# An RWKV-6 attention and squared-ReLU MLP kernel whose engines' order is planned anew

## The chip, the cores and the metric

The kernel runs on one core of a Trainium2 chip. The metric is device time in microseconds, the median of several executions. The core's engines are TensorE (PE, matmuls), VectorE (DVE), ScalarE (ACT), GpSimd (POOL) and SyncE (SP, which here issues every DMA transfer). Each engine works through its own list of instructions strictly in the order written; an instruction that waits holds up everything behind it on that engine.

## What is computed

A recurrent attention (4 batches, 8 heads, 768 time steps, head size 48) and behind it a two-layer network on its 3072 rows of 384 numbers:

```python
for t in range(S):
    cur = np.einsum('bhd,bhe->bhde', u[None] * kt, vt)
    y[:, :, t] = np.einsum('bhd,bhde->bhe', rt, state + cur)
    state = wt[:, :, :, None] * state + np.einsum('bhd,bhe->bhde', kt, vt)
x = y.transpose(0, 2, 1, 3).reshape(B * S, H * D)
r = np.maximum(x @ w_in, 0.0)        # w_in 384 x 2048
out = (r * r) @ w_out                # w_out 2048 x 384
```

All inputs and the output are float32.

## The kernel before

**Tiling.** The 768 time steps of a batch are cut into 6 chunks of 128, so there are 24 steps, numbered 0 to 23. A step handles all 8 heads of one chunk. The recurrence within a chunk becomes matrix products, and between the chunks of one batch a state S is handed on. Every batch starts with an empty state, so steps 0, 6, 12 and 18 have none to wait for.

**What a step does.** Each word below is a function that issues one or a few instructions. `ld:s:w`, `:r`, `:k`, `:v` load the step's four inputs (lines 149 to 165, 192 KB each). `lw` takes the logarithm of w (ACT, line 248); `cum` sums it over time by a matmul into the PSUM tile cp (line 276); `ci` makes the negated inclusive sum from it (DVE, line 282; steps 0 to 2 have a second matmul instead); `exp` exponentiates both halves (ACT, line 289); `rd` multiplies r and k by them (DVE, line 299). `tr` transposes the result (8 matmuls, line 308), `rkt` copies it out of PSUM, `p` forms the products of r and k (line 327), `pm0` and `pm1` mask them (DVE, line 339). `su`, `ac`, `ts` and `sn` bring the state forward (PE lines 350 to 357, ACT line 295, DVE line 362, the last on DVE or POOL). `ku`, `qp`, `q` and `vq` form the term with u. `ys` and `ye` are the matmuls that make the output y (lines 376, 387), `ysb` adds the u term (DVE, line 392), `yt` transposes (line 400), and `xt` copies the step's 128 columns into the big bf16 tile xT.

**The network.** The weights come in 4 groups each: `ld:g:i` and `ld:g:o` load 768 KB of w_in or w_out in float32 into one of six staging tiles w_st (lines 174 to 184), and `cast:i:g:j`, `cast:o:g:j` convert a piece to bf16. The tokens are handled in 17 blocks: blocks 0 to 8 and 16 hold one step, blocks 9 to 15 hold two. `m1:i:g` is a group of 12 matmuls of 128 columns, or 6 of 256, that fills one PSUM bank (line 418); `rl` takes the scaled ReLU out of it (ACT line 427 or DVE line 429), and `gt` squares it: on ACT (line 439), on DVE (line 441), or, with the letter W, on DVE from the ReLU and the bank itself (line 436). `m2:i:mt:q` is a quarter of the second product for 128 rows (4 matmuls of 384 columns, line 462); `os` scales it into an output tile and `store` writes it out. `oh` and `sh` do this for the last rows, in two pieces, and the last `m2` is split in two column ranges (line 458). `warm:n` issues matmuls on zeros that nobody reads (line 481).

**What sets the order.** The whole program is one list of 1125 words, `ORDER`, lines 16 to 98. A word's last letter says on which engine a movable step runs (A for ACT, V and W for DVE, G for POOL). The words are called one after the other under a manual schedule, so each engine's own list is the list's words of that engine, in that order:

```python
    with tc.manual_schedule(engines={E.PE, E.DVE, E.Activation, E.Pool, E.SP}):
        for word in ORDER.split():
            name, *args = word.split(":")
            todo[name](*(int(a) if a.isdigit() else a for a in args))
```

**What an engine can wait for.** Besides data, it is a buffer whose last reader is not done. The ones that matter here are few:

```python
    a_in = ctx.enter_context(tc.tile_pool(name="a_in", bufs=A_IN))            # 7 steps of inputs
    ps_cp = ctx.enter_context(tc.tile_pool(name="ps_cp", bufs=1, space=PSUM)) # cum, p
    ps_tr_pool = ctx.enter_context(tc.tile_pool(name="ps_tr", bufs=1, space=PSUM)) # tr, su, yt
    ps_m1 = ctx.enter_context(tc.tile_pool(name="ps_m1", bufs=2, space=PSUM)) # m1, warm
    ps_m2 = ctx.enter_context(tc.tile_pool(name="ps_m2", bufs=2, space=PSUM)) # m2
```

An `m1` therefore starts when the `rl` (and, with W, the `gt`) of the `m1` before the last has read its bank; a `tr`, `su` or `yt` starts when the one before it in the list has been read out.

## Time and profile before

| | us |
|---|---|
| runs of the kernel before | 191.91, 192.04, 192.87 |
| their median | 192.04 |
| the profiled execution | 193.03 |
| its span, first to last instruction | 191.2 |
| PE, DVE, ACT, POOL busy in it | 183.3, 153.5, 143.1, 81.0 |

The span is that of one profiled execution; 1.83 us of its time lie outside the span. "Busy" is the time that an engine's instructions cover; instructions of one engine overlap a little, and the end of a matmul is modelled, so a busy PE may still be waiting inside a row. L427 and the like are lines of the kernel.

### The profile page before, as it was taken

To read this page: it belongs to the slowest core of one execution; us is meant where nothing else is said; L and a number is where in the kernel's file an instruction comes from. 1 tells how busy PE (TensorE), PEld (TensorE's weight loads), DVE (VectorE), ACT (ScalarE), POOL (GpSimd) and SP (SyncE) were. 2 spreads that over 40 slices of the span, in tenths; PEclk is the share of its full clock that TensorE was granted. 3 is DMA by queue.
4 is the path that set the end of the run, shared out by engine and by line. 5 is a ranking of instruction groups with operands and counts; after the bars stand their busy time and mean duration, and the time that the engine had idled before them with its cause. 6 is when DMAs were issued, how large, how long until landed. Compare 5 with 4: busy or idle time off the path is not lost.

```text
span 191.2 us, 5444 instructions
## 1 busy us (share of the span) xinstructions
PE 183.3 (96%) x2172; PEld 139.1 (73%) x2172; DVE 153.5 (80%) x283; ACT 143.1 (75%) x283; POOL 81.0 (42%) x110
## 2 busy tenths in 40 slices
PE   7898799999999999999999999999999999999993
PEld 2345598877789778778869768778778778778773
DVE  3599887867999989999899989986688957967360
ACT  3554399995869979798969779958969968666530
POOL 6268274524377897925471484850032120000000
PEclk9999999999999999999999999999999999999999
DMA  6999989999999998999999899402002011002012
GB/s 131 218 222 258 367 229 332 373 186 219 186 249 191 195 211 167 249 212 242 213 238 227 168 241 184 141 3 82 3 0 82 3 41 46 0 2 86 0 45 82
DMA packets 107179, 30.24 MB, mean 158 GB/s; under 512 B 100369, under 2 KB 105618, under 8 KB 107154
## 3 DMA queue, kind: packets, MB, share of 16 engines
q1 hardware_dynamic: 107154, 29.89, 66.5%
q8 instruction: 17, 0.28, 0.6%
q14 instruction: 8, 0.07, 0.1%
HBM read 25.17 MB, written 4.72 MB: 156 GB/s over the span
## 4 chain that ended last, share of the span: by engine, by line
PE 80%; SPq 7%; ACT 6%; DMA 4%; issue 1%; DVE 0%; ACTq 0%
PE m L462 31%; PE m L418 31%; SPq L150 6%; PE tr L308 5%; DMA w_st<-in_moe_w_in_dram 4%; PE cp L327 3%; ACT rl L427 3%; PE y L387 2%; PE tr L400 2%; PE cp L276 2%; PE y L376 1%; PE tr L353 1%; ACT gt L439 1%; PE m L458 1%; ACT wi_sb L187 1%
## 5 line engine op out<-in xcount | busy, mean ns | idle before, releaser
L418 PE MATMUL m<-xT,wi_sb 128*128 128x128 bf16 (+1 forms) x816 | 74.7, 241 | 1.3 <-ACT wi_sb L187 0.9
L462 PE MATMUL m<-wo_sb,gt 128*128 128x384 bf16 x368 | 70.8, 326 | 0.0
L418 PEld LDWEIGHTS <-wi_sb 128*128 128x128 bf16 x816 | 59.5, 98 | 8.9 <-ACT wi_sb L187 1.1
L427 ACT ACTIVATE rl<-m 128x512 f16<-128x512 f32 x76 | 44.2, 596 | 13.7 <-PE m L418 12.7
L462 PEld LDWEIGHTS <-gt 128*128 128x128 bf16 x368 | 33.1, 98 | 16.5
L439 ACT ACTIVATE gt<-rl 128x512 bf16<-128x512 f16 x56 | 34.4, 630 | 1.6 <-DVE rl L429 0.9
L339 DVE TENSOR_TENSOR pmT<-cp,tri_strict 128x512 bf16<-128x512 f32 x42 | 27.2, 683 | 1.4 <-PE cp L327 1.3
L299 DVE TENSOR_TENSOR rdec_buf<-rk_raw,cp 128x768 bf16<-128x768 f32 x24 | 22.7, 948 | 4.7 <-ACT cp L289 4.5
L289 ACT ACTIVATE cp<-cp 128x768 f32<-128x768 f32 x24 | 19.2, 801 | 7.6 <-DVE cp L282 4.5
L190 POOL TENSOR_TENSOR qprod<-rk_raw,ku 128x384 f32<-128x384 f32 x19 | 19.6, 1033 | 11.4 <-DVE ku L190 5.4
L190 POOL TENSOR_TENSOR vq<-v_raw,q 128x384 f32<-128x384 f32 x20 | 16.9, 842 | 14.9 <-DVE q L264 7.9
L190 POOL TENSOR_TENSOR ku<-rk_raw,u_bc 128x384 f32<-128x384 f32 x19 | 20.2, 1064 | 0.3 <-issue 0.3
L190 POOL TENSOR_TENSOR S<-t_state,ac_buf 128x384 bf16<-128x384 f32 x11 | 9.4, 853 | 23.3 <-DVE t_state L362 23.3
L441 DVE TENSOR_TENSOR gt<-rl 128x512 bf16<-128x512 f16 x31 | 13.8, 447 | 6.4 <-ACT rl L427 6.3
L392 DVE TENSOR_TENSOR y_sb<-vq,y 128x384 bf16<-128x384 f32 x24 | 13.1, 548 | 4.0 <-PE y L387 4.0
L187 ACT COPY rkT<-tr 128x1024 bf16<-128x1024 bf16 x14 | 14.2, 1012 | 2.4 <-PE tr L308 2.4
L429 DVE TENSOR_SCALAR rl<-m 128x512 f16<-128x512 f32 x20 | 13.7, 688 | 2.7 <-PE m L418 2.3
L308 PE MATMUL tr<-ident,rdec_buf 128*128 128x128 bf16 x192 | 14.7, 219 | 0.5 <-ACT u_bc L187 0.2
L308 PEld LDWEIGHTS <-rdec_buf 128*128 128x128 bf16 x192 | 11.9, 98 | 3.2 <-issue 1.1
L248 ACT ACTIVATE lw_buf<-w_raw 128x384 bf16<-128x384 f32 x24 | 12.4, 522 | 2.2 <-POOL ac_buf L234 1.5
L282 DVE SCALAR_TENSOR_TENSOR cp<-cp,lw_buf 128x384 f32<-128x384 f32 x21 | 11.7, 559 | 2.6 <-PE cp L276 2.5
L264 DVE TENSOR_REDUCE q<-qprod 128x8 f32<-128x384 f32 x24 | 13.1, 545 | 0.6 <-POOL qprod L190 0.5
(67 smaller groups left out, 214.9 us busy)
## 6 DMA issues: line engine op xcount, KB each, us to landing
w_raw<-in_w_dram SPq DMA_DIRECT2D x24, 192.0 KB, 3.8
rk_raw<-in_r_dram SPq DMA_DIRECT2D x24, 192.0 KB, 3.7
rk_raw<-in_k_dram SPq DMA_DIRECT2D x24, 192.0 KB, 3.9
v_raw<-in_v_dram SPq DMA_DIRECT2D x24, 192.0 KB, 3.8
out_dram<-o_sb SPq DMA_DIRECT2D x23, 192.0 KB, 2.3
w_st<-in_moe_w_in_dram SPq DMA_DIRECT2D x4, 768.0 KB, 8.7
w_st<-in_moe_w_out_dram SPq DMA_DIRECT2D x4, 768.0 KB, 8.1
out_dram<-o_sb SPq DMA_DIRECT2D x1, 128.0 KB, 1.7
```

The lines of the kernel that those rows point to most:

```text
L187: {"A": nc.scalar.copy, "V": nc.vector.tensor_copy, "G": nc.gpsimd.tensor_copy}[eng](dst, src)
L190: {"V": nc.vector, "G": nc.gpsimd}[eng].tensor_mul(dst, a, b)
L289: nc.scalar.activation(cs[:, :, 0:DM], cs[:, :, 0:DM], AF.Exp)
L299: nc.vector.tensor_mul(rdec[:, :, :, 0:D], raw["rk", s][:], tiles.pop(("cs", s))[:, :, 0:DM].rearrange("p a (h d) -> p a h d", h=H))
L308: nc.tensor.transpose(ps_tr[:, i, p, :], rdec[:, i, 2 * p:2 * p + 2, :], ident[:])
L339: nc.vector.tensor_mul(tiles["pmT", s][:, e], tiles["p", s][e].rearrange("p (a t) -> p a t", a=HP), tri_strict[:, None, :].to_broadcast([C ...
L418: nc.tensor.matmul(ps1[:, j, :], wi_sb[:, kk, n * 128:(n + 1) * 128], xT[:, kk, s0 * C:s0 * C + width], start=(kk == 0), stop=(kk == KT - 1))
L427: nc.scalar.activation(rl[:], m1[:], AF.Relu, scale=RS)
L429: nc.vector.tensor_scalar(rl[:], m1[:], RS, 0.0, op0=ALU.mult, op1=ALU.max)
L439: nc.scalar.activation(gt, rl[:], AF.Square)
L441: nc.vector.tensor_mul(gt, rl[:], rl[:])
L462: nc.tensor.matmul(tiles["m2", i, mt][:], gt[:, n, mt * 128:(mt + 1) * 128], wo_sb[:, n, :], start=(n == 0), stop=(n == NT - 1))
```

## The change

Only the list changes. It has the same 1125 words with the same steps; what differs is their place, for some the engine letter, and the lengths of the 11 `warm` words (33.5 units of 512 columns in place of 34.5). Everything else in the file is the same.

```diff
 ORDER = """
-ld:0:w ld:0:r warm:6:1 ld:0:k ld:1:r ld:0:u lw:0 cum:0 ld:0:v warm:3:1 ld:1:w exp:0 ld:2:w rd:0 ub ld:2:r
...
+ld:0:w ld:0:r warm:6:1 ld:0:k ld:1:r ld:0:u lw:0 ld:0:v cum:0 ld:1:w warm:3 exp:0 ld:2:w rd:0 ld:2:r ub ld:1:k
...
```

The transfers keep their sequence for the first 35 words of SP, that is up to `ld:6:w` and the four that follow it. After that it differs: `ld:7:w`, `ld:8:w` and `ld:7:r` now come ahead of `ld:5:v` and `ld:6:v`, for instance, and the v inputs of steps 15 to 19 ahead of w of steps 14 and 15.

Between the engines this moves: ACT now has 69 of the 96 `rl` (76 before), 61 of the 96 `gt` (56 before), 18 `rkt` (14 before), 14 `v` (11 before), 12 `xt` (14 before) and 12 `cast:i`/`cast:o` (10 before). DVE has 27 `rl` (20 before), 35 `gt` of both kinds (40 before), 6 `rkt` (10 before), 12 `xt` (10 before), 2 `qp` (5 before) and 7 casts (6 before). POOL has 9 casts (12 before), 22 `qp` (19 before) and 9 `v` (13 before). One step is moved far: the last transpose `tr:23` stood 18 words ahead of `m1:15:0`, and stands 2 words behind it now.

**VectorE where the weights arrive.** Before, the stretch from the last `ysb` of the opening (step 2) on. rl and m are ReLU tile and `m1` bank, gt the squares, S and t_state the state, pmT the masked products, xT the transposed output, y_sb the step's output, q its u term.

```order
L392 TENSOR_TENSOR y_sb<-vq,y 128x384
L264 TENSOR_REDUCE q<-qprod 128x8
L429 TENSOR_SCALAR rl<-m_462 128x512
L339 TENSOR_TENSOR pmT<-cp,tri_strict 128x512
L441 TENSOR_TENSOR gt_461<-rl 128x512
L190 TENSOR_TENSOR S<-tr,ac_buf_133 128x384
L339 TENSOR_TENSOR pmT<-cp,tri_strict 128x512
L187 COPY xT<-tr 128x3x128
L441 TENSOR_TENSOR gt_501<-rl 128x512
L392 TENSOR_TENSOR y_sb<-vq,y 128x384
L362 TENSOR_TENSOR t_state<-S,tr 128x384
```

The same stretch of VectorE in the change, from the `ysb` of step 2 on:

```order
L392 TENSOR_TENSOR y_sb<-vq,y 128x384
L187 CAST wi_sb<-w_st 128x512
L429 TENSOR_SCALAR rl<-m_463 128x512
L339 TENSOR_TENSOR pmT<-cp,tri_strict 128x512 x2
L190 TENSOR_TENSOR S<-tr,ac_buf_133 128x384
L187 CAST wi_sb<-w_st 128x512
L429 TENSOR_SCALAR rl<-m_519 128x512
L441 TENSOR_TENSOR gt_476<-rl 128x512
L392 TENSOR_TENSOR y_sb<-vq,y 128x384
L187 COPY xT<-tr 128x3x128
L441 TENSOR_TENSOR gt_462<-rl 128x512
L282 SCALAR_TENSOR_TENSOR cp<-cp,lw_buf_125 128x384
```

Two casts of w_in pieces (`cast:i:1:0`, `cast:i:2:0`) now stand in VectorE's list, and a second ReLU, `rl:0:1`, behind them.

**ScalarE in the same place.** Before, from the four casts of w_in on (ac_buf is `ac`, lw_buf `lw`):

```order
L187 CAST wi_sb<-w_st 128x512 x4
L295 ACTIVATE ac_buf_133<-tr 64x4 x2
L427 ACTIVATE rl<-m_502 128x512
L439 ACTIVATE gt_501<-rl 128x512
L427 ACTIVATE rl<-m_522 128x512
L187 CAST wi_sb<-w_st 128x512
L427 ACTIVATE rl<-m_542 128x512
L295 ACTIVATE ac_buf_129<-tr 64x4 x2
```

In the change ScalarE has, from its third cast of w_in on:

```order
L187 CAST wi_sb<-w_st 128x512
L427 ACTIVATE rl<-m_477 128x512
L439 ACTIVATE gt_462<-rl 128x512
L295 ACTIVATE ac_buf_133<-tr 64x4 x2
L439 ACTIVATE gt_476<-rl 128x512
L427 ACTIVATE rl<-m_538 128x512
L248 ACTIVATE lw_buf_125<-w_raw 128x8x48
L427 ACTIVATE rl<-m_578 128x512
L427 ACTIVATE rl<-m_595 128x512
L295 ACTIVATE ac_buf_129<-tr 64x4 x2
L439 ACTIVATE gt_462<-rl 128x512
L427 ACTIVATE rl<-m_629 128x512
```

The logarithm of step 4, `lw:4`, has moved ahead of the ReLUs `rl:0:2` and `rl:1:2`, and two casts have left ScalarE here.

**VectorE in block 9.** Before, the stretch that begins with `rl:9:0`, the ReLU of the first group of block 9:

```order
L429 TENSOR_SCALAR rl<-m_1949 128x512
L471 TENSOR_SCALAR o_sb<-m_1869 128x384
L282 SCALAR_TENSOR_TENSOR cp<-cp,lw_buf_123 128x384
L441 TENSOR_TENSOR gt_1948<-rl 128x512
L187 COPY rkT<-tr 128x1024
L299 TENSOR_TENSOR rdec_buf_135<-rk_raw,cp 128x16x48
L190 TENSOR_TENSOR qprod<-rk_raw,ku 128x384
```

And in the change, from `ci:12`, the word ahead of it, on:

```order
L282 SCALAR_TENSOR_TENSOR cp<-cp,lw_buf_123 128x384
L429 TENSOR_SCALAR rl<-m_1955 128x512
L299 TENSOR_TENSOR rdec_buf_135<-rk_raw,cp 128x16x48
L187 COPY rkT<-tr 128x1024
L190 TENSOR_TENSOR ku<-rk_raw,u_bc 128x384
L282 SCALAR_TENSOR_TENSOR cp<-cp,lw_buf_125 128x384
L471 TENSOR_SCALAR o_sb<-m_1900 128x384
L441 TENSOR_TENSOR gt_1954<-rl 128x512
```

Step 13's `ci` comes into this stretch earlier; from the first `m1` of block 9 to the first of block 10 VectorE has 26 words in the list of the change, against 23 before.

160 lines of the change are left out of this document (80 added, 80 removed).

## The prediction

> **What bounds the kernel now.** I read the page's shares first, then the busy time stage by stage, then PE's own timeline where it loses time.
>
> ```profile
> PE 183.3 (96%) x2172; PEld 139.1 (73%) x2172; DVE 153.5 (80%) x283; ACT 143.1 (75%) x283; POOL 81.0 (42%) x110
> PE 80%; SPq 7%; ACT 6%; DMA 4%; issue 1%; DVE 0%; ACTq 0%
> core 0: us, PE busy (x) PEld busy (x) DVE busy (x) ACT busy (x) POOL busy (x), PEclk, DMA share, GB/s
> 22.93:34.23 11.30, 10.91 (x187) 9.88 (x188) 8.78 (x19) 10.01 (x23) 5.90 (x9) 1.00 0.95 296
> 43.17:86.52 43.35, 43.35 (x603) 34.38 (x602) 40.43 (x74) 36.42 (x75) 29.68 (x33) 1.00 1.00 209
> 86.52:100.39 13.87, 13.87 (x152) 10.62 (x150) 12.97 (x24) 11.13 (x23) 7.57 (x10) 1.00 1.07 231
> 100.39:115.16 14.77, 14.77 (x174) 11.35 (x173) 13.86 (x24) 12.37 (x26) 7.34 (x9) 1.00 1.05 213
> 115.16:188.13 72.97, 72.86 (x807) 56.64 (x804) 53.45 (x100) 53.83 (x104) 14.48 (x18) 1.00 0.16 48
> ```
>
> The chain of waits is PE for 80% of the span. From 43.17 on, PE is busy 144.85 of 144.96 us (the last four rows), until its last matmul ends at 188.13. The Trainium skill ("Perfetto Trace Analysis", section "Identifying the Most-Contended Engine") warns that matmul busy time is no measure of PE's headroom and takes weight-load busy time instead; by its 73% there would be a quarter of the span to win. So I looked at the starts of the matmuls, which nothing models.
>
> ```profile
> 22.41 0.23 PE L418 MATMUL m<-xT,wi_sb 128*128 128x128 bf16 x1 [0.61 <-ACT wi_sb L187]
> 22.93 0.79 PE L418 MATMUL m<-xT,wi_sb 128*128 128x128 bf16 x11 [0.29 <-ACT wi_sb L187]
> 23.65 0.40 PE L327 MATMUL cp<-rkT 64*128 64x128 bf16 x8
> 23.98 0.34 PE L350 MATMUL tr<-S,ident 128*128 128x384 bf16 x1
> ...
> 24.43 2.35 PE L418 MATMUL m<-xT,wi_sb 128*128 128x128 bf16 x36
> 26.61 0.33 PE L400 MATMUL tr<-ident,y_sb 128*128 128x128 bf16 x3
> 26.77 0.33 PE L376 MATMUL y<-S,rkT 128*128 128x96 bf16 x4
> 26.95 0.36 PE L387 MATMUL y<-v_bf,pmT 128*128 128x48 bf16 x8
> 27.39 0.33 PE L353 MATMUL tr<-v_bf,rdec_buf 128*128 128x96 bf16 x4
> 27.66 1.50 PE L418 MATMUL m<-xT,wi_sb 128*128 128x128 bf16 x24
> 29.00 0.33 PE L400 MATMUL tr<-ident,y_sb 128*128 128x128 bf16 x3
> 29.60 1.50 PE L418 MATMUL m<-xT,wi_sb 128*128 128x128 bf16 x24 [0.28 <-ACT rl L427]
> ```
>
> The 24 matmuls of 27.66 hand over at 29.00, 0.67 us per m1 group of 12; by the same reading p takes 0.33, su of step 2 0.45 (of step 3 0.27), yt, ys and cum some 0.17 each, ye about 0.2. Between 22.93 and 34.23, where the first m2 starts, PE does 12 groups (8.04 us), p:3, su:2, su:3, yt:2, yt:3, ys:3, ye:3 and cum:4 (1.93 us), together 9.97 us in 11.30. So 1.3 us are lost there, most of it inside busy rows, and nearly nothing after 43.17. What is ahead of 22.93 is bound by the arrival of w_in: the first group of weights must have landed and been cast.
>
> **The change, part by part.** *Ahead of the first m1: 0.* The words on PE ahead of `m1:0:0` are the same set in both lists apart from fillers, and the transfers come in the same sequence up to there.
>
> ```profile
> 18.05 1.30 SPq L150 DMA_DIRECT2D w_raw<-in_w_dram  x1
> DMA to landing us min/median/max: 10.1/10.1/10.1
> 21.74 1.14 ACT L187 CAST wi_sb<-w_st 128x512 bf16<-128x512 f32 x2 [1.57 <-DMA w_st<-in_moe_w_in_dram]
> 23.62 1.14 ACT L187 CAST wi_sb<-w_st 128x512 bf16<-128x512 f32 x2 [0.74 <-DMA w_st<-in_moe_w_in_dram]
> 32.22 0.77 POOL L187 CAST wo_sb<-w_st 128x384 bf16<-128x384 f32 x1 [2.17 <-DMA w_st<-in_moe_w_out_dram]
> ```
>
> The casts that waited for DMA show the landings: 21.72 and 23.6 for w_in, 32.2 for the first of w_out; `ld:4:w`, the first row, lands 10.1 us after its issue, at 28.15. Two casts of group 0 stay on ACT and one on POOL, so `m1:0:0` starts at 22.93 as before (only its first matmul, 22.41 before, now waits too: 0.05 us).
>
> *The weights' arrival, 22.93 to 34.23: 0 (from -1.3 to +0.8).* The durations:
>
> ```profile
> L339 DVE TENSOR_TENSOR pmT<-cp,tri_strict 128x512 bf16<-128x512 f32 x42 | 27.2, 683 | 1.4 <-PE cp L327 1.3
> L429 DVE TENSOR_SCALAR rl<-m 128x512 f16<-128x512 f32 x20 | 13.7, 688 | 2.7 <-PE m L418 2.3
> L441 DVE TENSOR_TENSOR gt<-rl 128x512 bf16<-128x512 f16 x31 | 13.8, 447 | 6.4 <-ACT rl L427 6.3
> L427 ACT ACTIVATE rl<-m 128x512 f16<-128x512 f32 x76 | 44.2, 596 | 13.7 <-PE m L418 12.7
> L439 ACT ACTIVATE gt<-rl 128x512 bf16<-128x512 f16 x56 | 34.4, 630 | 1.6 <-DVE rl L429 0.9
> L289 ACT ACTIVATE cp<-cp 128x768 f32<-128x768 f32 x24 | 19.2, 801 | 7.6 <-DVE cp L282 4.5
> 40.67 1.29 DVE L339 TENSOR_TENSOR pmT<-cp,tri_strict 128x512 bf16<-128x512 f32 x2
> ```
>
> Two maskings of 0.683 take 1.29: an instruction that waits for nothing starts some 0.08 us ahead of the end of the one before it. I use that on DVE and ACT, and 0.43 us for a w_in cast on DVE (none in the trace; estimated from its 0.35 for 384 columns).
>
> VectorE now stands at `cast:i:1:0` until 23.62; behind it are `rl:0:0` to 24.66, the masks of step 3 (p:3 is done at 24.65) to 25.95, `sn:2` to 26.42, `cast:i:2:0` to 26.77 and `rl:0:1` to 27.38. PE meanwhile: `m1:0:0`, `m1:1:0`, p:3 and su:2 to 25.10, `m1:0:1` and `m1:1:1` to 26.44, then yt:2, which needs the bank that `sn:2` reads until 26.42, just in time; ys:3 and ye:3 to 27.00. `m1:0:2` needs the bank that `rl:0:1` leaves at 27.38: **0.40 lost**. It and `m1:1:2` run to 28.74. ScalarE stands at `lw:4` until w of step 4 lands at 28.15, then has `lw:4` to 28.67, `rl:0:2` to 29.19, `rl:1:2` to 29.71, `ac:3`, `gt:0:2` and `rl:2:0` to 31.05, `rl:2:2` to 31.57, `exp:4` to 32.29, `rl:2:1` to 32.81. PE: cum:4 and su:3 to 29.17, `m1:2:0` at 29.21 (**0.04**), `m1:2:2` and yt:3 to 30.72, `m1:2:1` at 31.07 for the bank of `rl:2:0` (**0.35**), `m1:1:3` to 32.41, `m1:3:0` at 32.83 for the bank of `rl:2:1` (**0.42**), `m1:0:3` to 34.17. The first m2 waits for `cast:o:0:0`, the second of two on ACT behind `gt:2:0`: 34.22 (**0.07**). Together 1.28 us lost against 1.3 before: the first m2 starts at 34.24 in place of 34.23. The stall before `m1:2:2` and those around ACT's casts are gone, others stand in their place, since PE fills two banks faster than ACT and DVE empty them while they also cast. The ends: no loss at all, -1.3; and if ACT's ten instructions from 28.15 on got no overlap, 10 x 0.08 = +0.8. The hand schedule lies between, and I take it.
>
> *34.23 to 43.17: +0.1 (0 to 0.3).* Same work on PE. `m1:2:3` needs the bank that `gt:3:2:W` reads: `rl:3:2` on DVE to 36.90, the W another 0.69 to 37.6, where PE comes at 37.5.
>
> *From 43.17 to the last m1: +0.4 (0 to 1.8).* PE's own work is the same, and before it waited 0.11 us in all, so here the list can only lose. DVE has the least room, and at two places it gets more: 26 words for 23 from the first m1 of block 9 to that of block 10, and 42 words for 39 from the first m1 of block 5 to that of block 8.
>
> ```profile
> L299 DVE TENSOR_TENSOR rdec_buf<-rk_raw,cp 128x768 bf16<-128x768 f32 x24 | 22.7, 948 | 4.7 <-ACT cp L289 4.5
> 56.39:79.23 22.84, 22.84 (x319) 18.39 (x318) 21.64 (x39) 20.48 (x44) 19.36 (x22) 1.00 0.97 201
> L282 DVE SCALAR_TENSOR_TENSOR cp<-cp,lw_buf 128x384 f32<-128x384 f32 x21 | 11.7, 559 | 2.6 <-PE cp L276 2.5
> ```
>
> The 26 words of block 9 are 3 ci, 2 rd, 4 masks, 4 gt, one gt W (0.69), 2 q and 2 ysb (0.55 each) and one each of rl, rkt, ku, os, sn, ts, xt and vq (0.35 to 0.74, together 4.67): 15.6 us by their means. Counted the same way, the 42 words of blocks 5 to 7 make 26.0, and the 39 of before 24.6. Those 39 covered only 21.64 us of the row above, 0.88 of their sum, because they overlap; the 24 in block 9 of before come out at about the same share. At 0.88 the new words need 13.8 us in block 9 and 22.9 in blocks 5 to 7, where PE needs 14.1 (before 13.87, and one su more) and about 23.2 (22.84, and 0.4 of other small matmuls more). DVE would be covered to 98% at both places, where before it was to 94 and 95%. That is no bound yet, but there is no room for a late input either, so I put 0.2 us on each.
>
> *The transfers moved on SP's queue: 0.*
>
> ```profile
> 42.80 1.61 SPq L150 DMA_DIRECT2D v_raw<-in_v_dram  x2
> v_raw<-in_v_dram SPq DMA_DIRECT2D x24, 192.0 KB, 3.8
> ```
>
> The v of steps 5 and 6 now stand behind w of 7 and 8 and r of 7: three issues of some 0.8 us, so v of 5 is issued at about 45.2 and lands at 49. Its first readers, `v:5` and `vq:5`, stand in the list where PE has done some 50 us; ye:5 comes 3 us later, and that covers it. What is behind them on SP keeps at least 4 us to its first reader.
>
> *The end: 0.* The last matmuls of PE and the two last stores are the same words. The bank of the last block's m2 comes free by `os:15:0`, which now stands on ACT behind `gt:16:2`: 0.4 us ahead of PE by the overlapped durations. If that margin went, it would cost what is missing of it.
>
> **Sum.** 0 + 0 + 0.1 + 0.4 + 0 = +0.5 us on a span of 191.2. The profiled execution is 1.0 us above the median of the runs, so I add the difference to the median: 192.04 + 0.5 = **192.5 us**.
>
> **The rivals.** *VectorE becomes the bound in blocks 5 to 7 and 9 (slower).* If half of its overlap is lost, because its words wait for one another's results, block 9 takes halfway from 13.8 to 15.6, which is 14.7 against 14.1, and blocks 5 to 7 halfway from 22.9 to 26.0, 24.4 against 23.2: 0.6 + 1.2 = +1.8 in place of 0.4, 193.9 us. It decides from 14.1 / 26 = 0.54 and 23.2 / 42 = 0.55 us per word on; at the share of before they cost 0.53 and 0.54, without overlap 0.60 and 0.62. For it: that margin. Against it: 13.86 of 14.77 covered made no wait before. With waits of the same kind elsewhere, 0.30 that the kernel is slower by over 0.5%.
>
> *The opening's loss goes (faster).* If the waits for banks from 22.93 to 34.23 vanish, -1.3 on the 192.04, and with DVE keeping up, 190.8 us. For it: POOL and ACT stood waiting for landings before, so the old order did not fit them. Against it: two banks and the same landings, and four waits of my schedule. 0.07.
>
> *PE's clock falls in the opening (slower).* The first 7 fillers show it slow:
>
> ```profile
> 1.12 2.96 PE L481 MATMUL m<-warm 128*128 128x512 bf16 x7 [1.12 <-DVE warm L222]
> 9.88 1.25 PE L481 MATMUL m<-warm 128*128 128x512 bf16 x5
> ```
>
> 6.5 units take 2.96 us, 0.46 each, while 5 at 9.88 take 0.25 each. Fillers are moved, and if PE were slow again for 3 us of its work past 22.93, that would cost 1.5: 193.5 us. The longest gap of before, 0.61, did nothing, and the change has none that I find longer. The Trainium skill ("TensorE: Matmul & The Clock Gate", part 1) has the clock halved after an idle window of about 3.4 us, which speaks against this rival too; 0.02, within the 0.30 above.
>
> **How the numbers follow.** The measurement tells differences of about 0.5% (0.96 us) from no change: runs of the same kernel reach from 191.91 to 192.87. My forecast, +0.5 with its own range of 191.7 to 193.0, has 0.63 and lies inside that bound; slower has 0.30, faster 0.07. The range takes half of the opening's gain at the bottom (192.04 - 0.7 = 191.3) and the slower rival and half of the opening's 0.8 at the top (193.9 + 0.4 = 194.3).
>
> **What would show it.** PE's first m2 at 34.2 with waits ahead of `m1:0:2`, `m1:2:1` and `m1:3:0`; ACT idle until about 28.15 for `lw:4`; DVE covered for over 97% in block 9 and blocks 5 to 7, and PE waiting there by 0.1 to 0.6 us in all; the last matmul 188.3 to 189.0 us into the span. I am wrong if the first m2 comes before 33.5, if the landings shift, or if PE waits over 1 us anywhere past 43.

## The result, and the profile after

The change takes 194.86 us, the median of 194.08, 195.28, 194.43 and 195.87; the kernel before ran in 191.91 to 192.87 beside it, median 192.37. The ratio is 1.012 (95% interval 1.0079 to 1.0161): slower, by more than the scatter of the measurement and by less than 2%. Medians and ratios here and below leave out executions that lie over 1.5% above the fastest of their kernel: three of xt12_first, and one each of fill12, of open_new_rest_old (306.45 us) and of the kernel before. The forecast of 192.5 us was too low, and the time lies above its range of 191.3 to 194.3.

The profiled execution of the change took 194.08 us (span 192.3), the lowest of its four; that of before took 193.03 (span 191.2), the highest of its own. Their difference of 1.1 us therefore shows less than half of the 2.5 us between the medians. A second profile of the same kernel took 195.9 us (span 194.1). Both are read below: "first" and "second" profile of the change.

The page of the first: busy time, and the chain of waits.

```profile
PE 184.5 (96%) x2171; PEld 139.2 (72%) x2171; DVE 156.4 (81%) x283; ACT 147.5 (77%) x289; POOL 78.6 (41%) x104
PE 75%; ACT 9%; SPq 7%; DMA 3%; DVE 3%; issue 1%; ACTq 0%
```

TensorE (PE) is still the chain for most of the span, but ScalarE and VectorE now hold 12% of it, where before they held 6%. The forecast put VectorE's two full stretches at blocks 5 to 7 and block 9, so the windows are cut there again, from first projection to first projection: the first profile's blocks 5 to 7, block 9, block 10, and the rest up to the last matmul.

```profile
55.84:79.36 23.52, 23.46 (x329) 18.80 (x328) 23.03 (x42) 20.99 (x43) 15.25 (x16) 1.00 0.98 209
86.82:101.70 14.88, 14.32 (x158) 10.75 (x156) 14.29 (x27) 11.39 (x24) 6.78 (x8) 1.00 0.99 208
101.70:116.18 14.48, 14.48 (x165) 11.37 (x164) 12.21 (x21) 12.44 (x24) 7.89 (x10) 1.00 1.03 215
116.18:189.27 73.09, 73.09 (x810) 56.63 (x807) 54.81 (x98) 54.88 (x106) 15.18 (x18) 1.00 0.16 45
```

The same two stretches in the second profile:

```profile
56.53:81.18 24.65, 23.68 (x329) 18.87 (x328) 24.21 (x42) 21.05 (x43) 15.26 (x16) 1.00 0.89 188
88.64:103.52 14.88, 14.31 (x158) 10.74 (x156) 14.29 (x27) 11.38 (x24) 6.24 (x7) 1.00 1.04 211
```

The columns are the window's length, then PE, PEld, DVE, ACT and POOL busy. VectorE is covered 23.03 of 23.52 us and 14.29 of 14.88: 98% and 96%. Block 9 takes 14.88 us in both, 1.0 more than before, of which at most 0.3 is one more `su`. Blocks 5 to 7 take 23.52 in one and 24.65 in the other: a loss of 1.1 us that comes in some executions and not in others. From block 10 on nothing is lost.

What TensorE waited for between 43 and 190 us in the second profile (us in total, times, longest); the first has the latter row alone:

```profile
PE cp L276 <- DVE pmT L339: 1.0, 1, 1.0
PE m L418 <- ACT xT L187: 0.6, 1, 0.6
```

Since the ends of matmuls are modelled, such waits come out too short. To place the loss I used the starts alone. For each pair of neighbouring kinds of matmul, the tenth percentile of the distance between their starts, over the 18 profiles of this study, is taken as the pitch; what a distance has above it is called **stall** here. Summed over stretches of equal TensorE work (named by the times of before), in us, with the time at which the work of before's 44.3 us is done:

```
                      at 44   34-44  44-70  70-76  76-97  97-107 107-188
before                44.29   0.25   0.79   0.22   0.93   0.09   2.92
change, first         44.03   0.51   1.04   0.23   1.21   1.01   2.89
change, second        44.72   0.51   1.04   1.46   1.12   1.01   2.89
```

So past 44 us the change loses 1.4 us in the first profile and 2.6 in the second: 0.9 at the end of block 9 in both, 1.2 between 70 and 76 in the second alone, and 0.4 to 0.5 spread over the rest.

**The end of block 9.** TensorE before; cp<-rkT at 94.20 is `p:12`, y<-v_bf,pmT at 96.11 is `ye:12`, the last matmuls of step 12's output:

```profile
94.20 0.40 PE L327 MATMUL cp<-rkT 64*128 64x128 bf16 x8
...
96.11 0.36 PE L387 MATMUL y<-v_bf,pmT 128*128 128x48 bf16 x8
...
100.23 0.82 PE L418 MATMUL m<-xT,wi_sb 128*128 128x256 bf16 x6
```

The same place in the change, first profile, and below it the instructions of VectorE and ScalarE that the chain passes through:

```profile
96.97 0.40 PE L327 MATMUL cp<-rkT 64*128 64x128 bf16 x8
...
99.53 0.36 PE L387 MATMUL y<-v_bf,pmT 128*128 128x48 bf16 x8
...
99.90 0.81 PE L462 MATMUL m<-wo_sb,gt 128*128 128x384 bf16 x4
...
100.81 0.33 PE L400 MATMUL tr<-ident,y_sb 128*128 128x128 bf16 x3
101.70 1.47 PE L418 MATMUL m<-xT,wi_sb 128*128 128x256 bf16 x12 [0.57 <-ACT xT L187]
...
97.66 1.28 DVE L339 TENSOR_TENSOR pmT<-cp,tri_strict 128x512 bf16<-128x512 f32 x2
98.86 0.54 DVE L362 TENSOR_TENSOR t_state<-S,tr 128x384 f32<-128x384 bf16 x1
99.32 0.55 DVE L264 TENSOR_REDUCE q<-qprod 128x8 f32<-128x384 f32 x1
99.93 0.55 DVE L392 TENSOR_TENSOR y_sb<-vq,y 128x384 bf16<-128x384 f32 x1
100.40 0.35 DVE L187 COPY xT<-tr 128x384 bf16<-128x384 bf16 x1
101.17 0.48 ACT L187 COPY xT<-tr 128x384 bf16<-128x384 bf16 x1
```

`m1:10:0` needs the columns of step 12, and these come by a chain: `ye:12`, `ysb:12` on VectorE (99.93), `xt:11` (100.40), which frees the only bank for transposes, `yt:12` (100.81), `xt:12` on ScalarE (101.17). It takes 2.2 us from `ye:12` on. In the old list `ye:12` stood 4.1 us ahead of `m1:10:0`, with five quarters of m2 in between; in the new list one quarter is left, and TensorE runs out of work.

The chain begins further back, though. From `pm:12` on (97.66), which reads what `p:12` makes, VectorE has no gap of 0.1 us: `pm:12`, `ts:13`, `q:17`, `ysb:12`, `xt:11`. From `p:12` to `m1:10:0` it is 4.73 us, of which TensorE's own work takes some 3.9, counted as the time less the stall. In the old list it is 6.03 us, and TensorE has work for practically all of it.

**Between 70 and 76 us.** The second profile, VectorE, then GpSimd, and the matmul that waits:

```profile
71.87 1.09 DVE L190 TENSOR_TENSOR S<-t_state,ac_buf 128x384 bf16<-128x384 f32 x1
72.88 1.15 DVE L187 CAST v_bf<-v_raw 128x384 bf16<-128x384 f32 x1
73.95 0.54 DVE L190 TENSOR_TENSOR vq<-v_raw,q 128x384 f32<-128x384 f32 x1
74.42 1.27 DVE L339 TENSOR_TENSOR pmT<-cp,tri_strict 128x512 bf16<-128x512 f32 x2
...
71.54 1.00 POOL L190 TENSOR_TENSOR ku<-rk_raw,u_bc 128x384 f32<-128x384 f32 x1 [2.16 <-DMA rk_raw<-in_k_dram]
72.62 1.19 POOL L190 TENSOR_TENSOR qprod<-rk_raw,ku 128x384 f32<-128x384 f32 x1
...
75.75 0.34 PE L276 MATMUL cp<-lw_buf,tri_strict 128*128 128x384 bf16 x1 [0.97 <-DVE pmT L339]
```

The same instructions in the first profile, where nothing waited:

```profile
71.19 0.55 DVE L190 TENSOR_TENSOR S<-t_state,ac_buf 128x384 bf16<-128x384 f32 x1
71.65 0.35 DVE L187 CAST v_bf<-v_raw 128x384 bf16<-128x384 f32 x1
71.92 0.55 DVE L190 TENSOR_TENSOR vq<-v_raw,q 128x384 f32<-128x384 f32 x1
...
69.00 1.00 POOL L190 TENSOR_TENSOR ku<-rk_raw,u_bc 128x384 f32<-128x384 f32 x1 [0.30 <-DVE cp L282]
```

In the first, `ku:12` and, at 70.08, `qp:12` have begun on GpSimd before VectorE comes to `sn:8`, and nothing is held up. In the second, `ku:12` has to wait for k of step 12 and starts 2.5 us later; both fall together with `sn:8` and `v:10`, and these two take 1.09 and 1.15 us instead of 0.55 and 0.35; `cum:10` waits behind them for the bank that `pm:8` reads. In the old list, `sn:7` and `v:10` were not VectorE's.

The stall grows with the lateness of k. Seven profiles, those of the experiments included, have this piece of the new list unchanged: the first of the change, xt12_first, new_to_block8, fill_gt9, open_old_rest_new, the second of the change and fill12. In this order k of step 12 lands 2.3, 2.1, 1.4, 1.2, 0.6, 0.4 and 0.4 us ahead of `m1:7:0`, and the stall is 0.23, 0.23, 0.76, 0.92, 1.29, 1.46 and 1.46. What a mend does here can therefore be read only against a profile in which k is as late.

### The profile page after: what moved, and what is told of

It is laid out like the page before. It is cut to its first block, busy times and chain, and to the rows that moved or that the text cites. A ratio compares the mean times of both kernels' runs of the same rounds, so it can differ in the third digit from the quotient of the medians.

```text
span 192.3 us, 5413 instructions
## 1 busy us (share of the span) xinstructions
PE 184.5 (96%) x2171; PEld 139.2 (72%) x2171; DVE 156.4 (81%) x283; ACT 147.5 (77%) x289; POOL 78.6 (41%) x104
## 4 chain that ended last, share of the span: by engine, by line
PE 75%; ACT 9%; SPq 7%; DMA 3%; DVE 3%; issue 1%; ACTq 0%
PE m L462 29%; PE m L418 29%; SPq L150 6%; PE tr L308 4%; DMA w_st<-in_moe_w_in_dram 3%; PE cp L327 3%; ACT rl L427 3%; PE y L387 2%; ACT gt L439 2%; PE tr L353 2%; PE y L376 1%; PE tr L400 1%; PE cp L276 1%; ACT rkT L187 1%; ACT cp L289 1%
## 5 line engine op out<-in xcount | busy, mean ns | idle before, releaser
L427 ACT ACTIVATE rl<-m 128x512 f16<-128x512 f32 x69 | 40.2, 595 | 12.8 <-PE m L418 12.1
L462 PEld LDWEIGHTS <-gt 128*128 128x128 bf16 x368 | 33.5, 98 | 17.3 <-ACT gt L439 0.5
L439 ACT ACTIVATE gt<-rl 128x512 bf16<-128x512 f16 x61 | 37.9, 628 | 6.0 <-DVE rl L429 5.2
L190 POOL TENSOR_TENSOR qprod<-rk_raw,ku 128x384 f32<-128x384 f32 x22 | 22.2, 1011 | 9.4 <-DVE ku L190 7.0
L190 POOL TENSOR_TENSOR vq<-v_raw,q 128x384 f32<-128x384 f32 x19 | 16.3, 863 | 15.2 <-DVE y_sb L392 5.5
L190 POOL TENSOR_TENSOR ku<-rk_raw,u_bc 128x384 f32<-128x384 f32 x18 | 18.5, 1029 | 8.8 <-DMA rk_raw<-in_k_dram 8.5
L429 DVE TENSOR_SCALAR rl<-m 128x512 f16<-128x512 f32 x27 | 18.4, 685 | 3.1 <-PE m L418 2.9
L187 ACT COPY rkT<-tr 128x1024 bf16<-128x1024 bf16 x18 | 18.1, 1005 | 1.1 <-PE tr L308 1.1
L441 DVE TENSOR_TENSOR gt<-rl 128x512 bf16<-128x512 f16 x25 | 12.0, 481 | 8.2 <-ACT rl L427 8.2
L308 PE MATMUL tr<-ident,rdec_buf 128*128 128x128 bf16 x192 | 14.7, 219 | 0.4 <-ACT u_bc L187 0.3
L481 PE MATMUL m<-warm 128*128 128x512 bf16 (+1 forms) x36 | 11.1, 432 | 1.1 <-DVE warm L222 1.1
```

The lines of the kernel that those rows point to most:

```text
L187: {"A": nc.scalar.copy, "V": nc.vector.tensor_copy, "G": nc.gpsimd.tensor_copy}[eng](dst, src)
L190: {"V": nc.vector, "G": nc.gpsimd}[eng].tensor_mul(dst, a, b)
L308: nc.tensor.transpose(ps_tr[:, i, p, :], rdec[:, i, 2 * p:2 * p + 2, :], ident[:])
L427: nc.scalar.activation(rl[:], m1[:], AF.Relu, scale=RS)
L429: nc.vector.tensor_scalar(rl[:], m1[:], RS, 0.0, op0=ALU.mult, op1=ALU.max)
L439: nc.scalar.activation(gt, rl[:], AF.Square)
```

## The experiments

Each run was timed beside the kernel before on the same chip, and gave one profile; the ratios have intervals of 0.25 to 0.5% to either side, so a gain of a few tenths of a microsecond can show in a profile alone. Their stalls, in the columns of the table above, with the ratio to before and its interval:

```
                      at 44   34-44  44-70  70-76  76-97  97-107  ratio
after_again           44.72   0.51   1.04   1.46   1.12   1.01    1.0105 [1.0056, 1.0154]
open_new_rest_old     44.63   0.57   0.82   0.22   0.91   0.09    1.0033 [1.0008, 1.0057]
open_old_rest_new     44.57   0.38   1.04   1.29   1.11   1.01    1.0128 [1.0083, 1.0173]
xt12_first            44.50   0.51   1.04   0.23   1.21   1.01    1.0102 [1.0061, 1.0143]
fill12                44.41   0.51   1.49   1.46   1.11   0.85    1.0132 [1.0082, 1.0182]
dve_relief            44.35   0.51   1.03   0.71   1.11   1.01    1.0118 [1.0078, 1.0158]
fill_relief           45.60   0.51   1.04   0.27   1.16   0.85    1.0131 [1.0091, 1.0170]
oldopen_fill_relief   43.34   0.25   1.03   0.78   1.11   0.85    1.0083 [1.0049, 1.0116]
fill_gt9              44.13   0.51   1.04   0.92   1.11   0.74    1.0126 [1.0080, 1.0172]
vq10_late             44.42   0.51   1.04   0.89   1.11   1.01    1.0134 [1.0096, 1.0172]
all3                  44.19   0.51   1.04   0.89   1.11   0.74    1.0117 [1.0079, 1.0155]
oldopen_all3          43.43   0.25   1.04   0.89   1.11   0.74    1.0065 [1.0036, 1.0094]
new_to_block8         44.90   0.51   1.04   0.76   0.91   0.09    1.0078 [1.0047, 1.0108]
old_to_block8         44.34   0.25   0.80   0.22   1.70   1.01    1.0106 [1.0058, 1.0155]
hand_both             45.71   0.51   1.04   0.23   1.51   1.05    1.0118 [1.0083, 1.0153]
oldopen_hand          44.99   0.81   1.04   0.23   1.52   0.56    1.0068 [1.0034, 1.0101]
```

### Which part of the list

The change once more, as a control and for a second profile.

> The changed kernel once more, for a second profiled execution. Boundary theory (the loss is where block 10 begins, about 0.75 us of PE waiting for the copy xt:12, and some 0.5 us of small waits in blocks 5 to 9; all of it is in the first profile): 1.1 to 1.5 us above the kernel before, and the profile again has PE waiting for xT by 0.5 to 0.8 us near 101. Opening theory (the new order of the opening is more easily upset by when the transfers land, and the first profile was a lucky one): 2 to 3 us above the kernel before, with over 1 us more lost between 22 and 43 us than in the first profile.

195.5 us, ratio 1.0105, 2.5 us above the median of before. Its profile is the second one above. Neither theory has it whole: the wait for xT is there again (0.57), but the loss is more than the boundary theory's 1.1 to 1.5, and what comes on top of the first profile lies for the most part between 70 and 76 us (1.2), not in the opening, which ends 0.7 us later with the same stall between 34 and 44 (0.51).

The new list up to `m2:1:0:3` (about 43 us), then every word that is left in the old list's order and with its engine letters:

```diff
-(change) the new list to its end
+the new list to m2:1:0:3, then the old list
```

> The new list up to the last m2 of block 1 (about 43 us), then all other words in the old order and with the old engines. Boundary theory: as the kernel before, within 0.4 us. Opening theory: 1 to 2 us slower than the kernel before.

193.41 us, ratio 1.0033. No stall of the change past 44 us is left. The loss of 0.4 us by medians and 0.6 by the ratio is at the boundary theory's limit or just above it, and below what the opening theory needs.

The opposite splice, the old list up to `m2:1:0:3` and the new one behind it:

```diff
-(change) the new list to its end
+the old list to m2:1:0:3, then the new list
```

> The old list up to the last m2 of block 1, then all other words in the new order and with the new engines. Boundary theory: as slow as the change, 1.1 to 2.3 us above the kernel before, with PE waiting for xT near 101. Opening theory: not over 1.5 us above the kernel before.

195.61 us, ratio 1.0128, with the change's stalls at both places. So most of the loss lies past 43 us; the new opening costs 0.3 per cent, and the theory that the whole loss is the opening's falls.

Is `xt:12` late because `os:9:1`, the instruction in front of it on ScalarE, is?

```diff
-xt:11:V cum:14 vq:15:V os:9:1:A yt:12 ci:14 store:9:0 xt:12:A m1:10:0
+xt:11:V cum:14 vq:15:V yt:12 ci:14 store:9:0 xt:12:A os:9:1:A m1:10:0
```

> The changed list with one word moved: os:9:1 on ScalarE comes behind xt:12 in place of ahead of it. Boundary theory: 0.4 to 0.6 us faster than the change (the 0.49 us of os:9:1 no longer lies between yt:12 and the first m1 of block 10; what is left of the wait is the copy itself, about 0.5). Opening theory: the same gain, but 1 us or more still above the kernel before.

No: 195.05 us, 1.0102, and the stall at the end of block 9 stays at 1.01. The chain is late before it gets to ScalarE.

### Single mends

More TensorE work beside the chain: one quarter of m2 moved behind `yt:12`.

```diff
-ts:13 m2:9:0:3 ld:17:w q:17 sn:13:G ye:12 os:9:0:A yt:11 m2:9:1:3 ... os:9:1:A yt:12 ci:14 store:9:0 xt:12:A m1:10:0
+ts:13 ld:17:w q:17 sn:13:G ye:12 yt:11 m2:9:1:3 ... yt:12 m2:9:0:3 ci:14 xt:12:A os:9:1:A os:9:0:A store:9:0 m1:10:0
```

> The changed kernel, with m2:9:0:3 moved from in front of ye:12 to behind yt:12, and os:9:1, os:9:0 and store:9:0 behind xt:12. Theory A (half of the loss is the chain ye:12, ysb:12, xt:11, yt:12, xt:12 in front of m1:10:0, which the new list leaves with only three pieces of TensorE work beside it): the wait ahead of m1:10:0 goes from 0.57 to under 0.2 us, the work curve gains 0.7 to 1.0 us between 97 and 102, and the median comes out 0.7 to 1.0 us below the changed kernel's, about 194.3 to 194.6 on a chip where before gives 193.0. Rival B (xt:12 is late because ACT and DVE are full there, whatever PE does meanwhile): the wait stays over 0.4 and the median moves by less than 0.3.

195.27 us, ratio 1.0132: no gain. In its profile the wait ahead of `m1:10:0` is indeed gone, but TensorE reaches `yt:11` a quarter sooner, and now waits there for `ts:13` on VectorE, and at `yt:12` for `xt:11`, which stands behind `q:17` and `ysb:12`:

```profile
101.42 0.33 PE L400 MATMUL tr<-ident,y_sb 128*128 128x128 bf16 x3 [0.18 <-DVE t_state L362]
...
100.83 0.54 DVE L362 TENSOR_TENSOR t_state<-S,tr 128x384 f32<-128x384 bf16 x1
101.29 0.54 DVE L264 TENSOR_REDUCE q<-qprod 128x8 f32<-128x384 f32 x1
```

The stall falls by 0.16 only. A's wait went and B's median came: the stall moved on. The moved quarter lies between `p:12` and `m1:10:0` in both lists, so TensorE has no more work there than it had, and that distance only goes from 4.73 to 4.57 us. (The 1.49 between 44 and 70 lies ahead of the edit.)

Less work for VectorE around 70 us, as in the old list:

```diff
-sn:7:V ... v:10:V
+sn:7:G ... v:10:A
```

> The changed kernel with sn:7 back on GpSimd and v:10 back on ACT; nothing moves in the list. Theory C (the other half of the loss is VectorE held up between 66 and 74 us by GpSimd's ku, qprod and vq, when k of step 12 lands after 71): the wait of TensorE on pmT at 75 us is gone, no VectorE instruction of sn or v there takes over 0.9 us, the work curve loses under 0.4 us between 70 and 76 however late k of step 12 lands, and the median is 0.7 to 1.3 us below the changed kernel's. Rival D (the late k of step 12 itself delays the chain through qp:12 and q:12, with VectorE no part of it): where k of step 12 lands after 71 the loss between 70 and 76 stays at 1.0 to 1.3 us, and the median moves by less than 0.4.

195.06 us, ratio 1.0118: no gain that can be told, as rival D has it. In the profile the stall is 0.71. k lands 1.1 us ahead of `m1:7:0` there; with the list unchanged and k 1.2 us ahead (fill_gt9) it is 0.92, so only some 0.2 us are the edit's. The next instruction is now the one that is held up, `vq:10`, beside `qp:12`:

```profile
71.58 1.39 POOL L190 TENSOR_TENSOR qprod<-rk_raw,ku 128x384 f32<-128x384 f32 x1
72.02 1.36 DVE L190 TENSOR_TENSOR vq<-v_raw,q 128x384 f32<-128x384 f32 x1
74.64 0.34 PE L276 MATMUL cp<-lw_buf,tri_strict 128*128 128x384 bf16 x1 [0.23 <-DVE pmT L339]
```

Both edits, and both edits behind the old opening:

> Both edits together, of the kernel with m2:9:0:3 behind yt:12 and of the kernel with sn:7 on GpSimd and v:10 on ACT. If A and C both hold, the two gains add: 1.5 to 2.2 us below the changed kernel, which is 0 to 0.7 us over before (193.0 to 193.7 where before gives 193.0). If only one holds, 0.7 to 1.2 below the changed kernel. If the loss is spread over the whole of the new list, with the two places only where it shows, the time saved there is lost further on and the median stays within 0.4 of the changed kernel's.

> The list of before up to m2:1:0:3 (about 43 us), and from there the changed list with both edits. With the opening's price of about 0.4 us taken away too, A and C leave 192.9 to 193.4 where before gives 193.0: within 0.3 per cent of before. If what is left of the new list holds another loss that these edits do not touch, it is over 0.5 per cent slower than before; if the new list is better than the old one apart from the three places, it is faster by over 0.3 per cent.

195.41 us (1.0131) and 194.3 us (1.0083). The sum that was expected, 1.5 to 2.2 us, did not come; the time stays with the change's, as in the third reading of the first expectation. Behind the old opening the two mends bring 0.45 per cent against open_old_rest_new (1.0128), with intervals that overlap; behind the new one they bring nothing that can be measured.

Next, VectorE as the cause at the end of block 9: to fill12, two squares are added that go to ScalarE.

```diff
-gt:9:6:V ... gt:9:5:V
+gt:9:6:A ... gt:9:5:A
```

> The list of fill12 with gt:9:5 and gt:9:6 on ACT in place of VectorE (the engine that stands 1.1 us idle of 3 between 94 and 97 us in the changed kernel's profile, and 1.6 of 3 between 97 and 100). Theory E (the loss at the end of block 9 is VectorE's and not only the lack of TensorE work beside the chain: in fill12 the same 0.6 to 0.8 us came back as waits of yt:11 and yt:12 on VectorE): VectorE reaches ts:13 and ysb:12 0.5 to 0.8 us sooner, TensorE's time over its tightest pitch between yt:11 and m1:10:0 falls from 0.8 to under 0.4 us, and the median comes out 0.4 to 0.8 us below fill12's share, a ratio to before near 1.009. Rival F (the boundary costs a fixed time because the bank of the transposes is single, whoever does the squares): still 0.7 to 1.0, ratio 1.011 to 1.013.

195.42 us, ratio 1.0126; the stall at the end of block 9 is 0.74, for 0.85 in fill12. From `ye:12` to `m1:10:0` alone it is 0.56, for 0.68: more than E's 0.4 and less than F's 0.7, with F's ratio. `ts:13` comes only 0.13 us sooner (1.77 us behind `p:12`, in fill12 1.90), since it stands behind both halves of `pm:12`, which read what `p:12` makes.

And the order between 70 and 76: what is held up moved behind what TensorE waits for.

```diff
-sn:8:V lw:10 m1:7:0 v:10:V vq:10:V p:8 ... pm0:8 rl:7:0:A m1:7:2 ld:15:r pm1:8 ac:9
+sn:8:V lw:10 m1:7:0 p:8 ... pm0:8 rl:7:0:A m1:7:2 ld:15:r pm1:8 v:10:V vq:10:V ac:9
```

> The changed kernel with v:10 and vq:10 moved, on VectorE as before, from in front of both halves of pm:8 to behind them. Theory G (the 1.1 us between 70 and 76 is the two or three VectorE instructions that GpSimd holds up, standing in front of pm:8, on whose reading of the bank cum:10 waits; in dve_relief it was vq:10, 1.36 us for 0.55, that still stood there): the wait of TensorE at cum:10 is under 0.2 us whenever k of step 12 lands, the holding of v:10 and vq:10 is still seen but nothing waits for it, and the median is 0.5 to 1.2 us below the changed kernel's, a ratio near 1.006 to 1.009. Rival H (what comes late there comes late through q:12 or through v:10, which su:10 needs): the wait turns up at su:10, ye:10 or ysb:9 instead, and the ratio stays at 1.010 to 1.013.

195.51 us, ratio 1.0134. As theory G has it, `cum:10` waits no more; as H has it, the time does not fall. The stall turns up further on, at a place that neither named: `tr:9` needs the bank that `ts:9` reads, and `ts:9` now stands behind `v:10` and `vq:10`:

```profile
74.02 0.35 DVE L187 CAST v_bf<-v_raw 128x384 bf16<-128x384 f32 x1
74.28 0.55 DVE L190 TENSOR_TENSOR vq<-v_raw,q 128x384 f32<-128x384 f32 x1
74.75 0.55 DVE L362 TENSOR_TENSOR t_state<-S,tr 128x384 f32<-128x384 bf16 x1
75.35 0.61 PE L308 MATMUL tr<-ident,rdec_buf 128*128 128x128 bf16 x8 [0.50 <-DVE t_state L362]
```

These mends together, behind the new and the old opening:

> All edits: m2:9:0:3 behind yt:12 with the os:9 behind xt:12, gt:9:5 and gt:9:6 on ACT, v:10 and vq:10 behind pm:8. If E and G hold: TensorE's time over its tightest pitch is under 0.4 us at each of the two places, and the median is 1.3 to 1.9 us below the changed kernel's, a ratio of 1.001 to 1.005, the rest being the opening. If the loss wanders on to a third place: over 1.008.

> The list of before up to m2:1:0:3 (about 43 us), then the changed list with all those edits. E and G with the opening's 0.3 to 0.4 us taken back: a ratio of 0.998 to 1.002, no difference that can be measured. Over 1.006 would mean a loss past 43 us that these edits don't reach; under 0.996, that the new list is better than the old one apart from the places mended.

195.43 us (1.0117) and 194.08 us (1.0065). The ratio is that of a loss that wanders, but it wanders to no third place: it stays in the same two columns, 0.89 and 0.74, some instructions further on.

### Local, or the list as a whole

Two more splices, cut at the first projection of block 8 (79 us).

```diff
-(change) the new list to its end
+the new list up to m1:8:0, then the old list
```

> The changed list up to the first projection of block 8 (about 79 us), then the list of before. Theory I (the loss is local: two stretches in which TensorE stalls, 70 to 76 us and the end of block 9, and each goes with its own piece of the list): TensorE's stall between 70 and 76 us is 0.5 to 1.2 us more than before's, that at the end of block 9 is gone (0.1 or less, 0.03 in before's profile, 0.97 in the changed one), and the ratio to before is 1.004 to 1.009. Theory J (the loss belongs to the list as a whole, since less VectorE and GpSimd work is left to do late only if the early part is kept old): a stall turns up at the end of block 9 here too, ratio over 1.010.

194.31 us, ratio 1.0078; 0.76 us of stall at 70 to 76, and at the end of block 9 the 0.09 of before.

```diff
-(change) the new list to its end
+the old list up to m1:8:0, then the new list
```

> The list of before up to the first projection of block 8, then the changed list. Theory I: no more stall than before's between 70 and 76 us, 0.9 to 1.0 us at the end of block 9 and 0.1 to 0.3 on the way there, ratio 1.004 to 1.008; with new_to_block8's the two excesses add up to the changed kernel's 1.2 per cent within 0.3. Theory J: under 1.002 or over 1.010.

195.09 us, ratio 1.0106; 0.22 us at 70 to 76 as before, and 1.01 at the end of block 9. So each stall goes with its own piece of the list, as theory I says. The ratio does not fit I: 1.0106 is over its 1.008 and on J's side of the bound, and the sum misses, 0.78 and 1.06 per cent making 1.8, not 1.2. Some 0.5 us of it are the seam: the column 76-97 has 1.70 there, for 0.93 in the old and 1.1 to 1.2 in the new list.

Last, both places put in order for VectorE: all that TensorE waits for stands ahead of the rest.

```diff
-sn:7:V ... v:10:V vq:10:V p:8 ... pm1:8 ac:9 ku:12:G m1:7:1 gt:7:0:A ts:9
+sn:7:G ... v:10:A p:8 ... pm1:8 ac:9 ku:12:G m1:7:1 gt:7:0:A ts:9 vq:10:V
-gt:9:6:V ... gt:9:5:V p:12 v:14:G su:13 ysb:11 ld:20:r lw:14 m2:9:1:2 pm0:12 vq:14:G ac:13 m2:9:0:2 store:8:0 pm1:12
-lw:15 ld:16:w ts:13 m2:9:0:3 ld:17:w q:17 sn:13:G ye:12 os:9:0:A yt:11 m2:9:1:3 ysb:12 v:15:A ld:20:k xt:11:V
+gt:9:6:A ... gt:9:5:A p:12 v:14:G su:13 ac:13 ysb:11 ld:20:r lw:14 m2:9:1:2 pm0:12 ts:13 pm1:12 vq:14:G m2:9:0:2 yt:11 ye:12
+store:8:0 lw:15 ld:16:w ld:17:w sn:13:G m2:9:1:3 xt:11:V ysb:12 q:17 v:15:A ld:20:k
-cum:14 vq:15:V os:9:1:A yt:12 ci:14 store:9:0 xt:12:A m1:10:0
+cum:14 vq:15:V yt:12 m2:9:0:3 ci:14 xt:12:A os:9:1:A os:9:0:A store:9:0 m1:10:0
```

> The changed list with both places put in order for VectorE. At 70 to 76 us: sn:7 on GpSimd, v:10 on ACT, vq:10 behind ts:9, so that what GpSimd holds stands behind all that TensorE waits for. At the end of block 9: gt:9:5 and gt:9:6 on ACT, ts:13 in front of the second half of pm:12, yt:11 in front of ye:12, xt:11 in front of ysb:12 and q:17 behind it, m2:9:0:3 behind yt:12, the os:9 behind xt:12. Theory K (the stalls are VectorE's: not its share of the stretch but what stands in front of ts, pm, ysb and xt in its queue): 0.3 us or less of stall over before's at each place, ratio 1.003 to 1.007. If the stalls stay at 0.6 us or more each, as in the two runs that moved one obstacle only, VectorE's order is not what sets them: ratio 1.010 or more.

> The list of before up to m2:1:0:3, then the list of hand_both. Theory K: a ratio of 0.999 to 1.004, hand_both's less 0.2 to 0.4 per cent. Without K: near 1.007, as in the run with the first mends and the old opening.

195.15 us (1.0118) and 194.5 us (1.0068): theory K's numbers do not come; the second is what was expected without K. Its first half holds in the profiles: at 70 to 76 us the stall is before's (0.23 for 0.22), with `vq:10` behind `ts:9`. oldopen_hand shows it, since k lands only 0.5 us ahead of `m1:7:0` there and the unchanged list would lose some 1.3; with it rival D falls, since k is late and the stall is gone. In hand_both k is 2.0 us ahead, and there would have been little to mend. Its rows:

```profile
75.31 0.55 DVE L362 TENSOR_TENSOR t_state<-S,tr 128x384 f32<-128x384 bf16 x1
75.77 0.55 DVE L190 TENSOR_TENSOR vq<-v_raw,q 128x384 f32<-128x384 f32 x1
...
77.91 1.09 PEld L462 LDWEIGHTS <-gt 128*128 128x128 bf16 x8 [0.38 <-DVE gt L436]
```

But a weight load of m2 at 77.91 then waits for a square that VectorE makes after all this, and the column 76-97 grows by 0.3 to 0.4, of which 0.16 of stall is at this quarter. At the end of block 9 the stall is halved (0.37 between `ye:12` and `m1:10:0` in both profiles, for 0.83; another 0.49 of hand_both's falls behind `m1:10:0`). With the old opening the stall past 44 us sums to 6.25 us (2.90 of it past 107), against 7.34 in open_old_rest_new and 4.95 in before.

No version beats the kernel before; the nearest is open_new_rest_old.

## Why the prediction was wrong

**The step that failed is "From 43.17 to the last m1: +0.4 (0 to 1.8)".** It put 0.2 us on each of two stretches, blocks 5 to 7 and block 9, and nothing elsewhere. Measured past 44 us: +1.4 in one profile and +2.6 in the other. Three things are in it.

- *Block 9* was mis-sized: it took 14.88 us, 0.8 over the 14.1 that the step gave TensorE, and not 0.2. The step counted VectorE's words against the length of the stretch, 13.8 of 14.1 us. It came out at 14.29 us, but that share is not what sets the wait: xt12_first, fill12, fill_gt9 and hand_both shorten the chain or VectorE's queue, and each leaves 0.5 to 1.0 us. What a count of words cannot see is a distance in the list: from `ye:12` to `m1:10:0` 4.1 us in the old list and 2.2 in the new, from `p:12` to `m1:10:0` 6.0 and 4.7. The chain through VectorE, one bank and ScalarE needs 4.73, 4.57, 4.46 and 4.27 us from `p:12` on in the change, fill12, fill_gt9 and hand_both, and TensorE has some 3.9 us of work beside it in all four, so no edit gave it more work there. This is read from the profiles; no mend took the whole stall away. That the old piece of list alone removes it (new_to_block8, 0.09) is shown; which of its moves suffices is not. A list in which `p:12` itself comes earlier was not tried.
- *Blocks 5 to 7* were mis-sized by execution: 23.52 us in the first profile, about the step's 23.2 and 0.2, and 24.65 in the second, 1.2 more. That the first agrees is the luck of an early k of step 12. The step counted words by their means. The trace of before has `vq` on VectorE spread widely (ns, least, median and most of four), and what makes some of them long was not followed up:

```profile
L190 DVE TENSOR_TENSOR vq<-v_raw,q x4: 549/720/973, 75.4 to 148.8; 128x384 f32<-128x384 f32 x4
```

Two more words that can be held up, `v:10` and `vq:10`, now stand in front of `pm:8`, and whether they are hangs on when k of step 12 lands.
- *Elsewhere* 0.4 to 0.5 us came in pieces of 0.05 to 0.25, for instance 0.24 at a quarter of m2 at 86.00 in the first profile. The step had nothing for them.

**"The transfers moved on SP's queue: 0"** failed with it. "At least 4 us to its first reader" is no margin, since a landing takes 3.8 us by the prediction's own row. In the kernel before, k of step 12 landed at 68.58 and GpSimd came to `ku:12` at 70.16, 1.6 us later. In the first profile of the change it is 4.0 us from the issue to `ku:12` (65.01 to 69.00), and the landing takes 3.9 of them. In the second the issue comes at 67.64, and `ku:12` waits 2.16 us. It stands behind v of steps 9 and 10 and w of steps 10 and 11 on SP. Its issue in the first profile:

```profile
65.01 1.53 SPq L150 DMA_DIRECT2D rk_raw<-in_k_dram  x1
```

and in the second:

```profile
67.64 0.76 SPq L150 DMA_DIRECT2D rk_raw<-in_k_dram  x1
```

GpSimd itself has time to spare; but what it does late, it does beside VectorE.

**Ahead of the first m1 and the weights' arrival, 0 and 0:** the first m2 was forecast at 34.24 and came at 33.72 and 34.41, so within what executions differ by. The first profile's waits:

```profile
28.20 0.32 PE L276 MATMUL cp<-lw_buf,tri_strict 128*128 128x384 bf16 x1 [0.33 <-ACT lw_buf L248]
30.68 1.50 PE L418 MATMUL m<-xT,wi_sb 128*128 128x128 bf16 x24 [0.25 <-ACT rl L427]
32.38 1.50 PE L418 MATMUL m<-xT,wi_sb 128*128 128x128 bf16 x24 [0.20 <-ACT rl L427]
...
27.63 0.52 ACT L248 ACTIVATE lw_buf<-w_raw 128x384 bf16<-128x384 f32 x1 [1.35 <-DMA w_raw<-in_w_dram]
```

The waits at 30.68 and 32.38 are those forecast ahead of `m1:2:1` and `m1:3:0`, and ScalarE did stand idle for `lw:4`, 1.35 us. Of the 0.40 forecast ahead of `m1:0:2` the starts show 0.2; the wait at `cum:4`, behind that `lw:4`, was not forecast, and the second profile does not have it. The whole new opening costs 0.33 per cent, 0.6 us (open_new_rest_old), of which 0.26 to 0.32 are stall between 34 and 44, where the forecast had 0.1 (0 to 0.3): ahead of `m1:2:3`, the place that it named, the change's profiles have 0.27. For the other 0.3 us the runs name no cause.

**The end, 0:** right. From the last matmul's start to the end of the execution it is 5.03 and 5.04 us, for 5.13 before.

**The rivals.** "VectorE becomes the bound in blocks 5 to 7 and 9" was the nearest, with 193.9 us and 0.30: the places and the engine are right, and its 24.4 and 14.7 us for the two stretches lie near the second profile's 24.65 and 14.88. Its mechanism is not: it had half of VectorE's overlap lost because its words wait for one another. The overlap was kept: VectorE's covered time is 0.88 to 0.89 of the sum of its instructions in blocks 5 to 7 in both profiles, and 0.90 to 0.91 in block 9, where the rival needs 0.94. Blocks 5 to 7 are longer in the second because GpSimd holds instructions up, so the agreement in size is luck. A bound by busy time would also yield to an engine swap, and here each swap moved the stall a few instructions on. The opening's loss did not go. The clock did fall in the opening, but ahead of the work that this rival put its price on, and no cost of it is clear of the scatter (last section).

**What stays open:** why the mends bring 0.45 to 0.63 per cent behind the old opening (against open_old_rest_new, by medians) and nothing measurable behind the new one. It may be scatter: the intervals of open_old_rest_new and of each of these mends overlap, as do those of hand_both and oldopen_hand, and the profiles show the same stalls past 76 us but for 0.49 us right after the start of block 10.

## What to carry to other kernels

When a list without slack is reordered, look for each chain that ends in the bottleneck engine, measure its length through the other engines, and count the bottleneck's work between the two ends: if the list leaves less work than the chain is long, the difference is lost, however busy the engines are on average. Take the chain from its first link: counted from `ye:12`, one more quarter of m2 looked like a mend; counted from `p:12`, it added no work. Where an engine was covered to 96 to 98%, as VectorE here, the time saved at one instruction was mostly waited for at the next. And take a duration from its slowest row, not its mean, where another engine can hold it up.
